# Two MLPs behind a packed attention: a pair of PSUM banks of their own for the small products, their latest input first, loads tied to steps

## The chip, the cores and the metric

The kernel runs on one core of a Trainium2 chip. The number that counts is the device time of one execution in microseconds (us): the median of three runs of the kernel before is 851.89 us (850.17 to 852.31). TensorE multiplies matrices (PE in the profile), VectorE (DVE) and ScalarE (ACT) work on elements, GpSimd (POOL) issues a few DMAs and SyncE (SP) most of them. PSUM, which TensorE writes its products to, has eight banks; a bank here holds 128 partitions by 512 float32 numbers.

## The reference

```python
def sm_attn(qq, kk, vv):
    s = scale * np.matmul(qq, kk.transpose(0, 1, 3, 2))
    s = s - np.max(s, axis=-1, keepdims=True)
    a = np.exp(s)
    a = a / (np.sum(a, axis=-1, keepdims=True) + 1e-09)
    return np.matmul(a, vv)
p_packed = sm_attn(p, k, v)             # p: [4, 8, 32, 64]; q, k, v: [4, 8, 576, 64], float32
x = sm_attn(q, p_packed, p_packed)      # then packed to [2304, 512]
h = x @ w_in                            # 512 x 2048, float64 weights
x = (h * np.tanh(log1p(exp(h)))) @ w_out   # 2048 x 512: first MLP (Mish)
h = x @ w_in2                           # second MLP, the same shapes, ELU
out = np.where(h > 0.0, h, np.exp(np.minimum(h, 0.0)) - 1.0) @ w_out2
```

## The kernel before

**The large products.** Each of the four large matrix products is made as three products of parts (high by high, high by low, low by high), so that its precision is that of float32. The float64 weights arrive as pairs of 32-bit words. ACT (L135) and DVE (L138, L143, L148) decode them into float32, and `split` (L163 on ACT, L165 or L167 on DVE) makes the high and the low part. The stages follow one another: `startup` (attention of batch 0, first decoded weights), `mixture1` (the first MLP, 128 steps of 288 tokens by 128 hidden columns), `mixture2` (the second MLP, 80 steps, 16 for each block of 512 or at last 256 tokens). Step i of mixture1 is `gemm1(i)` (L445 to L447, 6 products), `mish(i)` (ACT L454 and L455, DVE L456) and `gemm2(i-2)` (L473 to L475, 12 products). Step i of mixture2 is `gemm3` (L536 to L538, 12 products) one step ahead, its ELU (ACT L540, DVE L541 and L542, then the split L163 and L165), and `gemm4` (L559 to L561).

**The small products.** Attention and the folds run on TensorE in tiles of 32x32 or 64x32 of its array, where several instructions for different tiles go side by side. For each batch b they are: `scores1` (L244, p by k; kT from DVE's transpose L224), `transpose_a1` (L288), `packed` (L313, then L335 or L337), `scores2` (L354, q by the packed values; qT from L224 as well) and four times `fold` (L414), which multiplies the packed values into 512 columns of the first MLP's weights. What a fold leaves is the left operand G[b, c] of gemm1, so that gemm1 needs only the softmax of scores2 (`turn_s`, `exps`, `norm`, `back`: tiles x, a2t, a2h, a2l) on its other side. A small product has a "pe" step and "post" steps, which read its PSUM tile.

**PSUM before.** `ps_a` holds two tiles of two banks, the accumulators of gemm2 and gemm4. `ps_h` holds four single banks, taken in turn by gemm1, by gemm3 and, two at a time, by `pm()` for every small product.

**What sets the order.** Two tracks, `att` and `fol`, hold the small products of batches 1 to 3 with the step from which each may start; at each step of mixture1 a track takes one step of its current product. Loads of k, v and q of the next batch are issued at fixed steps (LOADOFF), folds of batch 0 at the steps of F0. The order in which the code emits instructions is not the order on the engines: a scheduler of the framework, with a model of times, reorders them as their inputs, tiles and banks come free. A tile of the `small` pool (nine slots) or of `up` (29) must be released by its last reader before it is taken again.

Of the kernel before, what the change touches and what calls it, by code (L numbers as in the profile page):

```python
# [20 lines left out]
    F0=[0, 14, 19],  # L21
# [8 lines left out]
    LOADOFF=[-2, 4, 0, 6, 11, 12],  # L30
# [13 lines left out]
def kernel(  # L44
# [19 lines left out]
    NK = DFF // 128  # L64
# [15 lines left out]
    ps_h = ctx.enter_context(tc.tile_pool(name="ps_h", bufs=4, space=bass.MemoryType.PSUM))  # L80
# [10 lines left out]

    def pm():
        if starting[0]:
            turn[0] += 1
            if turn[0] % 2:
                t = ps_a.tile([128, 2, 512], F32, tag="acc", name="pm")
                return [t[:, 0, :], t[:, 1, :]]
        return [ps_h.tile([128, 512], F32, tag="h", name="pm") for _ in range(2)]
# [135 lines left out]
    def scores1(b, s):  # L234
        d = {}

        def pe():
            ps = d["ps"] = pm()
            for x in range(2):
                for g in range(4):  # L240
                    kg = kT[b, g].rearrange("p e s -> p (e s)").rearrange("p (j x t) -> p j x t", x=2, t=32)
                    for th in range(2):
                        r = 64 * s + 32 * th
                        nc.tensor.matmul(  # L244
                            out=ps[th][32 * g:32 * g + 32, 0:HALF],
                            lhsT=pT[r:r + 32, b * 4 + g, x, :],
                            rhs=kg[r:r + 32, :, x, :],
                            start=(x == 0),
                            stop=(x == 1),
                        )  # L250
            if s:
                for g in range(4):
                    kT.pop((b, g))

        def post1():
            sm = d["sm"] = st.tile([128, 6], F32, tag="sm", name="sm")
            for e in range(2):
                nc.vector.reduce_max(out=sm[:, 2 + e:3 + e], in_=d["ps"][e][:, 0:HALF], axis=AX.X)
            nc.vector.tensor_scalar(
                out=sm[:, 1:2], in0=sm[:, 2:3], scalar1=sm[:, 3:4], scalar2=-scale, op0=ALU.max, op1=ALU.mult  # L260
            )
            e1 = E1[b, s] = small([128, 2, HALF], F32, f"e1_{b}_{s}")
            for e in range(2):
                nc.scalar.activation(
                    out=e1[:, e, :].rearrange("p (t j) -> p j t", t=32),
                    in_=d["ps"][e][:, 0:HALF].rearrange("p (j t) -> p j t", t=32), func=ACTF.Exp,
                    bias=sm[:, 1:2], scale=scale, accum_out=sm[:, 4 + e:5 + e],
                )

        def post2():  # L270
            sm = d["sm"]
            rs = RS[b, s] = st.tile([128, 2], F32, tag="rs", name="rs")
            nc.vector.tensor_scalar(
                out=rs[:, 0:1], in0=sm[:, 4:5], scalar1=sm[:, 5:6], scalar2=1e-9, op0=ALU.add, op1=ALU.add
            )
            nc.vector.reciprocal(out=rs[:, 1:2], in_=rs[:, 0:1])

        return [pe, post1, post2]
# [26 lines left out]
    def packed(b, s):  # L305
        d = {}

        def pe():
            a1 = A1T.pop((b, s))
            ps = d["ps"] = pm()  # L310
            for i, w, _, _ in CHUNKS:
                for g in range(4):
# [32 lines left out]
    def scores2(b):  # L345
# [3 lines left out]
        def pe(e):  # L349
            ps = d[e] = pm()  # L350
            for g in range(4):
# [34 lines left out]
        def back(s):  # L386
# [11 lines left out]
            lambda: (turn_s(1), exps(0)),  # L398
# [7 lines left out]
    def fold(b, c):  # L406
        d = {}

        def pe():
            ps = d["ps"] = pm()  # L410
            for g in range(4):
# [116 lines left out]
    def gemm3(j, kk):  # L528
        n = blocks[j][1]
        h = ps_h.tile([128, 512], F32, tag="h", name="h2")  # L530
        hp = h[:, 0:n]
# [46 lines left out]
    def attention_steps(b):  # L578
        st = [transpose_heads(kt_in, kT, b, g, "kT") for g in range(4)]
        st += [scores1(b, s) for s in range(2)]  # L580
        st += [transpose_a1(b, s, P["EVA"][s]) for s in range(2)]
        st += [packed(b, s) for s in range(2)]
        st += [transpose_heads(qt_in, qT, b, g, "qT") for g in range(4)]
        return st + [scores2(b)]
# [37 lines left out]
    def startup():  # L622
# [26 lines left out]
        def filler(m):  # L649
# [8 lines left out]
        hk, hq, s2 = at[0:4], at[10:14], at[14]  # L658
# [5 lines left out]
            6, hq[0][0], hq[1][0], hq[2][0], hq[3][0], s2[0], s2[1], s2[2], s2[3], 8, f0[0], f0[1],  # L664
            s2[4], s2[5], 45,
# [10 lines left out]
    class Track:  # L676
# [7 lines left out]

        def start(self, i):
# [4 lines left out]
    def mixture1():  # L690
# [3 lines left out]
        for b in range(1, B):  # L694
# [7 lines left out]
            for off, f in (  # L702
                (P['LOADOFF'][0], lambda b=b: load_kt(k, kt_in, b, 0, "k")),
                (P['LOADOFF'][1], lambda b=b: load_vt(b, 0)),
                (P['LOADOFF'][2], lambda b=b: load_kt(k, kt_in, b, 1, "k")),
                (P['LOADOFF'][3], lambda b=b: load_vt(b, 1)),
                (P['LOADOFF'][4], lambda b=b: load_kt(q, qt_in, b, 0, "q")),
                (P['LOADOFF'][5], lambda b=b: load_kt(q, qt_in, b, 1, "q")),
            ):
                at.setdefault(max(a0 - 1 + off, 0), []).append(f)  # L710
# [4 lines left out]
        fold0 = {F0[c - 1]: fold(0, c) for c in range(1, 4)}  # L715
        fposts = []
        for i in range(NA + LAG):
            for f in fposts:
                f()
            fposts = []  # L720
# [3 lines left out]
            att.posts()  # L724
            if i < NA:
# [7 lines left out]
            if i in fold0:  # L733
                fold0[i][0]()
                fposts.append(fold0[i][1])
            if FAST0 <= i < 2 * NK:
                att.posts()
                if not fol.cur and not att.cur:
# [5 lines left out]
            if not fol.cur and not att.cur:  # L744
# [77 lines left out]
```

## Time and profile before

| what | value |
|---|---|
| median of three runs | 851.89 us (850.17 to 852.31) |
| the profiled execution | 850.69 us |
| its span, from first to last instruction | 848.6 us |
| PE busy | 794.7 us (94%) |
| DVE busy | 441.4 us (52%) |
| ACT busy | 355.5 us (42%) |
| mean granted clock of TensorE | 0.963 of full speed |
| mean DMA rate | 94 GB/s |

The profile page divides the span into 40 slices. TensorE is nearly always busy from the fifth slice on, and has most of its idle time in the first four. The busy time of the second to the fourth slice is what DVE, ACT and the loads have to do before there is a first large product. The page's fifth part lists groups of instructions by line. The product lines of the four large products carry nearly all of TensorE's time: L473 to L475 appear 512 times each, L536 to L538 320 times and L559 to L561 288 times.

### The profile page before, as it was taken

The page shows a single profiled execution, that of the slowest core. Times are in us where ns is not written, and L with a number is a line of the kernel's source. Part 1 is how long each engine was busy: PE and PEld are TensorE (multiplying, and loading weights), DVE is VectorE, ACT ScalarE, POOL GpSimd, SP SyncE. Part 2 cuts the span into 40 slices and gives each one's busy share as a digit, 9 for nine tenths or more (in the row PEclk, how much of TensorE's full clock was granted, in tenths as well). Part 3 has the DMA queues.
Part 4 walks back from the last instruction along what each step waited for, and adds up shares of the span by engine and source line. Part 5 has one row for each costly group of instructions (what it writes and reads, how often), then busy time and mean ns, then how long its engine had stood idle before and what let it go on. Part 6 is the DMA issues. An engine that isn't in the chain of part 4 may idle for free.

```text
span 848.6 us, 12983 instructions
## 1 busy us (share of the span) xinstructions
PE 794.7 (94%) x5172; PEld 672.4 (79%) x5172; DVE 441.4 (52%) x860; ACT 355.5 (42%) x678; POOL 14.1 (2%) x30
## 2 busy tenths in 40 slices
PE   4508899999999999999998999999999999999997
PEld 3207687799878898699996888888888888888886
DVE  2789787823463335545617999523352334333443
ACT  1355665636374545556436565322231223222222
POOL 0000000000000000000000000000000000000000
PEclk7658899999999999999999999999999999999999
DMA  8996483443223332522106453200020001000000
GB/s 208 292 392 187 151 254 82 111 168 56 79 81 125 93 50 93 184 78 76 43 12 209 144 172 96 92 12 1 1 75 13 1 1 37 26 1 1 31 21 25
DMA packets 86044, 80.01 MB, mean 94 GB/s; under 512 B 63712, under 2 KB 68320, under 8 KB 85984
## 3 DMA queue, kind: packets, MB, share of 16 engines
q1 hardware_dynamic: 76704, 69.16, 26.3%
q0 software_dynamic: 2432, 8.91, 2.8%
q10 hardware_dynamic: 6848, 1.11, 0.7%
q8 instruction: 40, 0.66, 0.3%
q14 instruction: 20, 0.16, 0.1%
HBM read 65.54 MB, written 13.63 MB: 93 GB/s over the span
## 4 chain that ended last, share of the span: by engine, by line
PE 48%; issue 39%; DMA 4%; DVE 3%; ACT 2%; SPq 2%; POOL 1%; ACTq 0%; POOLq 0%; DVEq 0%
PE o L559 8%; PE o L560 8%; PE o L561 8%; PE h L536 7%; PE h L538 7%; PE h L537 7%; DMA raw_w1o<-in_moe_w_out_dram 1%; DMA v<-in_v_dram 1%; POOL y_dr L489 1%; DMA pr<-in_p_dram 1%; SPq L201 1%; DVE dec L143 1%; SPq L111 1%; PE acc L474 1%; DMA raw_w2i<-in_moe_w_in_dram 1%
## 5 line engine op out<-in xcount | busy, mean ns | idle before, releaser
L474 PE MATMUL acc<-gl,w1oh 128*128 128x288 f32 x512 | 151.0, 297 | 0.0
L475 PE MATMUL acc<-gh,w1ol 128*128 128x288 f32 x512 | 150.0, 295 | 0.0
L473 PE MATMUL acc<-gh,w1oh 128*128 128x288 f32 x512 | 148.8, 301 | 0.3
L536 PE MATMUL h<-yh,w2ih 128*128 128x512 f32 (+1 forms) x320 | 117.0, 369 | 2.7 <-ACT yh L163 1.4
L537 PE MATMUL h<-yl,w2ih 128*128 128x512 f32 (+1 forms) x320 | 118.0, 369 | 0.0
L538 PE MATMUL h<-yh,w2il 128*128 128x512 f32 (+1 forms) x320 | 117.3, 368 | 0.0
L559 PE MATMUL o<-w2oh,gh 128*128 128x512 f32 x288 | 112.5, 390 | 0.7 <-ACT ob L212 0.7
L560 PE MATMUL o<-w2ol,gh 128*128 128x512 f32 x288 | 112.4, 390 | 0.0
L540 ACT ACTIVATE t<-h 128x512 f32<-128x512 f32 (+1 forms) x80 | 44.2, 553 | 156.0 <-PE h L538 155.8
L456 DVE TENSOR_TENSOR gl<-t,gh 128x288 fp32r<-128x288 f32 x128 | 57.8, 453 | 96.6 <-ACT gh L455 96.4
L445 PE MATMUL h<-a2h,gh 128*128 128x288 f32 x256 | 80.8, 317 | 27.8 <-ACT a2h L163 23.9
L541 DVE TENSOR_SCALAR t<-t 128x512 f32<-128x512 f32 (+1 forms) x80 | 32.0, 399 | 142.6 <-ACT t L540 142.6
L473 PEld LDWEIGHTS acc<-gh,w1oh 128*128 128x128 f32 x512 | 95.2, 190 | 11.8 <-issue 8.3
L561 PE MATMUL o<-w2oh,gl 128*128 128x512 f32 x288 | 104.1, 390 | 0.0
L474 PEld LDWEIGHTS acc<-gl,w1oh 128*128 128x128 f32 x512 | 96.7, 189 | 4.9 <-issue 1.9
L475 PEld LDWEIGHTS acc<-gh,w1ol 128*128 128x128 f32 x512 | 96.6, 189 | 0.0
L454 ACT ACTIVATE t<-h 128x288 f32<-128x288 f32 x128 | 52.1, 409 | 102.2 <-PE h L447 100.2
L445 PEld LDWEIGHTS h<-a2h,gh 128*128 128x128 f32 x256 | 49.3, 193 | 45.2 <-ACT a2h L163 25.1
L163 ACT ACTIVATE gh<-t 128x512 fp32r<-128x512 f32 (+1 forms) x80 | 47.0, 587 | 73.2 <-DVE t L542 51.5
L446 PE MATMUL h<-a2l,gh 128*128 128x288 f32 x256 | 77.2, 302 | 0.1
L447 PE MATMUL h<-a2h,gl 128*128 128x288 f32 x256 | 76.8, 301 | 0.0
L165 DVE TENSOR_TENSOR gl<-t,gh 128x512 fp32r<-128x512 f32 (+1 forms) x80 | 51.0, 637 | 43.7 <-ACT gh L163 43.6
(96 smaller groups left out, 1144.7 us busy)
## 6 DMA issues: line engine op xcount, KB each, us to landing
w1r<-w_dr SPq DMA_DIRECT2D x24, 512.0 KB, 4.7
raw_w1i<-in_moe_w_in_dram SPq DMA_DIRECT2D x16, 512.0 KB, 6.9
raw_w1o<-in_moe_w_out_dram SPq DMA_DIRECT2D x16, 512.0 KB, 10.2
raw_w2i<-in_moe_w_in_dram SPq DMA_DIRECT2D x16, 512.0 KB, 4.8
raw_w2o<-in_moe_w_out_dram SPq DMA_DIRECT2D x16, 512.0 KB, 4.4
k<-in_k_dram SPq DMA_DIRECT2D x16, 288.0 KB, 5.8
y_dr<-y POOLq DMA_DIRECT2D x16, 288.0 KB, 2.6
out_dram<-ob SPq DMA_DIRECT2D x18, 256.0 KB, 2.0
```

Source lines behind the costliest of these rows:

```text
L445: nc.tensor.matmul(out=hp, lhsT=wh, rhs=xh, start=(kt == 0), stop=False)
L446: nc.tensor.matmul(out=hp, lhsT=wh, rhs=xl, start=False, stop=False)
L447: nc.tensor.matmul(out=hp, lhsT=wl, rhs=xh, start=False, stop=(kt == 1))
L473: nc.tensor.matmul(out=o, lhsT=wh[:, cs], rhs=gh, start=first, stop=False)
L474: nc.tensor.matmul(out=o, lhsT=wh[:, cs], rhs=gl, start=False, stop=False)
L475: nc.tensor.matmul(out=o, lhsT=wl[:, cs], rhs=gh, start=False, stop=last)
L536: nc.tensor.matmul(out=hp, lhsT=wh, rhs=xh, start=(i == 0), stop=False)
L537: nc.tensor.matmul(out=hp, lhsT=wh, rhs=xl, start=False, stop=False)
L538: nc.tensor.matmul(out=hp, lhsT=wl, rhs=xh, start=False, stop=(i == 3))
L559: nc.tensor.matmul(out=o, lhsT=gh[:, ts], rhs=wh, start=(kk == 0), stop=False)
L560: nc.tensor.matmul(out=o, lhsT=gh[:, ts], rhs=wl, start=False, stop=False)
L561: nc.tensor.matmul(out=o, lhsT=gl[:, ts], rhs=wh, start=False, stop=(kk == NK - 1))
```

## The change

It has six parts. (1) `ps_h` shrinks from four banks to two. The two freed banks become one tile, `ps_p`, that `pm()` gives to every small product after startup; in startup two turns of three take an accumulator of `ps_a`. `gemm3` uses all four banks through `hbank`: of four steps the first two take the two banks of ps_h, the third takes the pair and its first half, the fourth its second half. (2) The loops over the four head pairs in scores1, packed, scores2 and fold run from 3 down to 0. (3) The loads of v are issued with the second pe step of scores1, those of q with the pe steps of packed; LOADOFF is gone. (4) scores2 is two products for the track instead of one: the transposes out of PSUM in the first, the softmax in the second. (5) The folds of batch 0 stand in the `fol` track, at steps 0, 12 and 17, and a fold may also start ahead of gemm1. (6) `att` doesn't start a product while a fold is due.

```diff
-    ps_h = ctx.enter_context(tc.tile_pool(name="ps_h", bufs=4, space=bass.MemoryType.PSUM))
+    ps_h = ctx.enter_context(tc.tile_pool(name="ps_h", bufs=2, space=bass.MemoryType.PSUM))
+    ps_p = ctx.enter_context(tc.tile_pool(name="ps_p", bufs=1, space=bass.MemoryType.PSUM))
...
     def pm():
-        if starting[0]:
-            turn[0] += 1
-            if turn[0] % 2:
-                t = ps_a.tile([128, 2, 512], F32, tag="acc", name="pm")
-                return [t[:, 0, :], t[:, 1, :]]
-        return [ps_h.tile([128, 512], F32, tag="h", name="pm") for _ in range(2)]
+        turn[0] += 1
+        if starting[0] and turn[0] % 3:
+            t = ps_a.tile([128, 2, 512], F32, tag="acc", name="pm")
+        else:
+            t = ps_p.tile([128, 2, 512], F32, tag="pm", name="pm")
+        return [t[:, 0, :], t[:, 1, :]]
+
+    spare = []
+
+    def hbank(n):
+        if n % 4 < 2:
+            return ps_h.tile([128, 512], F32, tag="h", name="h2")
+        if n % 4 == 2:
+            spare.append(ps_p.tile([128, 2, 512], F32, tag="pm", name="h2"))
+            return spare[0][:, 0, :]
+        return spare.pop()[:, 1, :]
...
# in scores1, packed, scores2 and fold
-                for g in range(4):
+                for g in (3, 2, 1, 0):
...
         return [
             lambda: pe(0),
             lambda: (turn_s(0), pe(1)),
-            lambda: (turn_s(1), exps(0)),
+            lambda: turn_s(1),
+        ], [
+            lambda: exps(0),
             lambda: exps(1),
             lambda: (norm(0), back(0)),
             lambda: (norm(1), back(1)),
...
# gemm3
-        h = ps_h.tile([128, 512], F32, tag="h", name="h2")
-        hp = h[:, 0:n]
+        hp = hbank(j * NK + kk)[:, 0:n]
...
# attention_steps
+        for s in range(2):
+            x = scores1(b, s)
+            if s:
+                x[0] = then(x[0], lambda: load_vt(b, 0), lambda: load_vt(b, 1))
+            st.append(x)
...
+            x = packed(b, s)
+            x[0] = then(x[0], lambda s=s: load_kt(q, qt_in, b, s, "q"))
...
+        st += scores2(b)
...
# mixture1, inside the loop over the steps
             fol.posts()
             att.posts()
+            if not fol.cur and not att.cur:
+                fol.start(i)
             if i < NA:
                 gemm1(i)
...
-                if not fol.cur and not att.cur:
+                if not fol.cur and not att.cur and not fol.due(i):
                     att.start(i)
```

How this moves instructions on TensorE in the first small product of batch 1 (pm is its PSUM tile, kT1_0 to kT1_3 are the transposed heads of k, acc and h1 the tiles of gemm2 and gemm1). Before, the first scores1 begins like this:

```order
L473 MATMUL acc0_612<-gh1_669,w1oh4_0_520 128x288
L473 MATMUL acc1_613<-gh1_669,w1oh4_0_520 128x288
L244 MATMUL pm_833<-kT1_0_692,pT_94 32x288
L244 MATMUL pm_834<-kT1_0_692,pT_94 32x288
L244 MATMUL pm_833<-kT1_1_719,pT_94 32x288
L244 MATMUL pm_834<-kT1_1_719,pT_94 32x288
L474 MATMUL acc0_612<-gl1_670,w1oh4_0_520 128x288
L475 MATMUL acc0_612<-gh1_669,w1ol4_0_521 128x288
L473 MATMUL acc0_612<-gh1_669,w1oh4_0_520 128x288
```

It goes on in three further pieces with ten to twelve large products between them. In the changed kernel it stands in one piece, with a large product ahead of it and behind it:

```order
L461 MATMUL h1_692<-a2h0_431,gl0_1_563 128x288
L256 MATMUL pm_821<-kT1_3_783,pT_97 32x288 x2
L256 MATMUL pm_821<-kT1_2_750,pT_97 32x288 x2
L256 MATMUL pm_821<-kT1_1_717,pT_97 32x288 x2
L256 MATMUL pm_821<-kT1_0_690,pT_97 32x288 x2
L256 MATMUL pm_821<-kT1_3_783,pT_97 32x288 x2
L256 MATMUL pm_821<-kT1_2_750,pT_97 32x288 x2
L256 MATMUL pm_821<-kT1_1_717,pT_97 32x288 x2
L256 MATMUL pm_821<-kT1_0_690,pT_97 32x288 x2
L459 MATMUL h1_719<-a2h0_431,gh0_1_562 128x288
```

There all 16 instructions, two to a row, follow one another; kT1_3 comes first.

On VectorE in startup, the softmax behind the second scores (x0_0 and x0_1 are its scores, w1v and w1ol decoded weights, gl0_0 a part of the first fold). Before, from the last transposes out of PSUM:

```order
L368 STREAM_TRANSPOSE x0_1_380<-pm_383 128x288
L167 SCALAR_TENSOR_TENSOR gl0_0_422<-pm_412,gh0_0_421 128x512
L375 TENSOR_REDUCE mx2_394<-x0_0_378 128x18
L375 TENSOR_REDUCE mx2_398<-x0_1_380 128x18
L167 SCALAR_TENSOR_TENSOR w1ol0_0_449<-dec_447,w1oh0_0_448 128x512
L148 SCALAR_TENSOR_TENSOR w1v1_0_459<-raw_w1i0_1_196,dec_458 128x512
L148 SCALAR_TENSOR_TENSOR w1v1_2_467<-raw_w1i2_1_198,dec_466 128x512
L376 TENSOR_TENSOR x0_0_378<-x0_0_378,mx2_394 128x576
L167 SCALAR_TENSOR_TENSOR gl0_0_422<-pm_412,gh0_0_421 128x512
L376 TENSOR_TENSOR x0_1_380<-x0_1_380,mx2_398 128x576
L138 TENSOR_SCALAR dec_474<-raw_w1i1_1_200 128x512
L138 TENSOR_SCALAR dec_482<-raw_w1i3_1_202 128x512
```

In the changed kernel, from the same place:

```order
L380 STREAM_TRANSPOSE x0_1_380<-pm_382 128x288
L387 TENSOR_REDUCE mx2_393<-x0_0_378 128x18
L387 TENSOR_REDUCE mx2_397<-x0_1_380 128x18
L388 TENSOR_TENSOR x0_0_378<-x0_0_378,mx2_393 128x576
L388 TENSOR_TENSOR x0_1_380<-x0_1_380,mx2_397 128x576
L393 TENSOR_REDUCE sm2_426<-x0_0_378 128x18
L393 TENSOR_REDUCE sm2_437<-x0_1_380 128x18
L394 TENSOR_SCALAR sm2_426<-sm2_426 128x18
L394 TENSOR_SCALAR sm2_437<-sm2_437 128x18
L395 RECIPROCAL sm2_426<-sm2_426 128x18
L179 SCALAR_TENSOR_TENSOR gl0_0_421<-pm_411,gh0_0_420 128x512
L395 RECIPROCAL sm2_437<-sm2_437 128x18
```

The steps of the softmax follow one another up to the reciprocal and beyond, and the two parts of the fold and the decodes that stood between them come later.

On TensorE where mixture2 begins (h2 is the tile of gemm3; yh and yl are its right operand). Before, this is where the fourth gemm3 ends and the fifth begins:

```order
L536 MATMUL h2_5429<-yh0_1_5100,w2ih2_0_4289 128x512
L537 MATMUL h2_5429<-yl0_1_5101,w2ih2_0_4289 128x512
L538 MATMUL h2_5429<-yh0_1_5100,w2il2_0_4290 128x512
L536 MATMUL h2_5462<-yh0_0_5096,w2ih0_1_5107 128x512
L537 MATMUL h2_5462<-yl0_0_5097,w2ih0_1_5107 128x512
L538 MATMUL h2_5462<-yh0_0_5096,w2il0_1_5108 128x512
```

In the changed kernel the fifth, h2_5421, stands behind the third, h2_5356:

```order
L549 MATMUL h2_5356<-yh0_1_5060,w2ih2_0_4249 128x512
L550 MATMUL h2_5356<-yl0_1_5061,w2ih2_0_4249 128x512
L551 MATMUL h2_5356<-yh0_1_5060,w2il2_0_4250 128x512
L549 MATMUL h2_5421<-yh0_0_5056,w2ih0_1_5067 128x512
L550 MATMUL h2_5421<-yl0_0_5057,w2ih0_1_5067 128x512
L551 MATMUL h2_5421<-yh0_0_5056,w2il0_1_5068 128x512
```

The fourth, which takes the second half of tile h2_5356, comes behind the first products of the second gemm4 (gh2_5338):

```order
L572 MATMUL o0_5342<-w2oh0_0_4294,gh2_5338 128x512
L573 MATMUL o0_5342<-w2ol0_0_4295,gh2_5338 128x512
L572 MATMUL o1_5343<-w2oh0_0_4294,gh2_5338 128x512
L573 MATMUL o1_5343<-w2ol0_0_4295,gh2_5338 128x512
L549 MATMUL h2_5356<-yh0_0_5056,w2ih0_0_4204 128x512
L574 MATMUL o0_5342<-w2oh0_0_4294,gl2_5339 128x512
```

So three gemm3 products instead of four are done before the first bank is needed again.

## Rows read from the trace of the kernel before

**Rows 1.** Stretches of 20 us: busy us and count by engine, PEclk, DMA share, GB/s

```profile
40.00:60.00 20.00, 0.00 (x0) 0.00 (x0) 15.73 (x33) 10.66 (x18) 1.06 (x2) 0.52 1.03 411
60.00:80.00 20.00, 15.14 (x87) 12.54 (x88) 19.38 (x36) 12.17 (x24) 0.00 (x0) 0.71 0.63 198
...
100.00:120.00 20.00, 18.32 (x157) 15.48 (x157) 15.23 (x33) 14.15 (x27) 1.20 (x2) 0.86 0.59 171
...
240.00:260.00 20.00, 19.86 (x147) 13.89 (x146) 11.65 (x23) 11.85 (x25) 0.00 (x0) 1.00 0.28 93
...
380.00:400.00 20.00, 20.00 (x154) 20.00 (x153) 13.44 (x28) 13.39 (x30) 0.00 (x0) 1.00 0.36 114
```

**Rows 2.** Waits of PE: us in total, times, longest us

```profile
PE h L445 <- ACT a2h L163: 23.9, 1, 23.9
PE h L445 <- ACT t L454: 3.0, 2, 2.7
```

**Rows 3.** Timeline of PE at scores1 of batches 1 and 2: start, us, instruction

```profile
84.53 0.69 PE L244 MATMUL pm<-kT,pT 32*32 32x288 f32 x8
85.15 0.40 PE L474 MATMUL acc<-gl,w1oh 128*128 128x288 f32 x1
85.39 0.30 PE L475 MATMUL acc<-gh,w1ol 128*128 128x288 f32 x1
85.52 0.29 PE L473 MATMUL acc<-gh,w1oh 128*128 128x288 f32 x1
...
86.57 0.42 PE L473 MATMUL acc<-gh,w1oh 128*128 128x288 f32 x2
86.92 0.68 PE L244 MATMUL pm<-kT,pT 32*32 32x288 f32 x6
...
195.11 1.20 PE L244 MATMUL pm<-kT,pT 32*32 32x288 f32 x32
196.24 0.40 PE L445 MATMUL h<-a2h,gh 128*128 128x288 f32 x1
```

**Rows 4.** Timeline of PE at three folds

```profile
113.23 1.06 PE L414 MATMUL pm<-w1v,pt 64*32 64x512 f32 x8
114.22 0.40 PE L473 MATMUL acc<-gh,w1oh 128*128 128x288 f32 x1
...
165.69 1.09 PE L414 MATMUL pm<-w1r,pt 64*32 64x512 f32 x16
166.71 0.40 PE L445 MATMUL h<-a2h,gh 128*128 128x288 f32 x1
...
241.56 1.91 PE L414 MATMUL pm<-w1r,pt 64*32 64x512 f32 x4
243.40 0.40 PE L474 MATMUL acc<-gl,w1oh 128*128 128x288 f32 x1
```

**Rows 5.** Timeline of PE at a piece of scores2 of batch 1

```profile
135.83 1.15 PE L354 MATMUL pm<-qT,pt 64*32 64x288 f32 x6
136.91 0.40 PE L474 MATMUL acc<-gl,w1oh 128*128 128x288 f32 x1
```

**Rows 6.** Timelines of ACT and DVE in startup

```profile
43.55 0.65 ACT L135 ACTIVATE raw_w1o<-raw_w1o 128x512 f32<-128x512 f32 x1 [1.63 <-DMA raw_w1o<-in_moe_w_out_dram]
...
44.71 0.69 DVE L167 SCALAR_TENSOR_TENSOR gl<-pm,gh 128x512 fp32r<-128x512 f32 x1 [4.27 <-ACT gh L163]
...
65.84 0.76 DVE L165 TENSOR_TENSOR a2l<-a2t,a2h 128x576 fp32r<-128x576 f32 x1
```

**Rows 7.** Timelines of DVE and PE at the start of mixture2

```profile
460.47 0.68 DVE L542 SCALAR_TENSOR_TENSOR t<-h,t 128x512 f32<-128x512 f32 x1
...
459.32 0.39 PE L537 MATMUL h<-yl,w2ih 128*128 128x512 f32 x1
459.55 0.39 PE L538 MATMUL h<-yh,w2il 128*128 128x512 f32 x1
461.20 0.50 PE L536 MATMUL h<-yh,w2ih 128*128 128x512 f32 x1 [1.26 <-DVE t L542]
```

More of the change, by code (lines that the diff above doesn't have):

```diff
@@ L20 @@
     DEC1=[14, 26],
-    F0=[0, 14, 19],
+    F0=[0, 12, 17],
     LEAD=2,
@@ L29 @@
     RELOFF=-7,
-    LOADOFF=[-2, 4, 0, 6, 11, 12],
     NU=29,
@@ L311, in pe @@
             for i, w, _, _ in CHUNKS:
-                for g in range(4):
+                for g in (3, 2, 1, 0):
                     nc.tensor.matmul(
@@ L350, in pe @@
             ps = d[e] = pm()
-            for g in range(4):
+            for g in (3, 2, 1, 0):
                 for s in range(2):
@@ L410, in pe @@
             ps = d["ps"] = pm()
-            for g in range(4):
+            for g in (3, 2, 1, 0):
                 for s in range(2):
@@ L578, in attention_steps, with then, both @@
     def attention_steps(b):
-        st = [transpose_heads(kt_in, kT, b, g, "kT") for g in range(4)]
-        st += [scores1(b, s) for s in range(2)]
+        def then(f, *loads):
+            def both():
+                f()
+                for x in loads if b else ():
+                    x()
+            return both
+        st = [transpose_heads(kt_in, kT, b, g, "kT") for g in range(4)]
+        for s in range(2):
[3 more added lines that the diff above has]
+            st.append(x)
         st += [transpose_a1(b, s, P["EVA"][s]) for s in range(2)]
-        st += [packed(b, s) for s in range(2)]
+        for s in range(2):
+            x = packed(b, s)
+            x[0] = then(x[0], lambda s=s: load_kt(q, qt_in, b, s, "q"))
+            st.append(x)
         st += [transpose_heads(qt_in, qT, b, g, "qT") for g in range(4)]
-        return st + [scores2(b)]
+        st += scores2(b)
+        return st
     NA = 2 * B * NK
@@ L657, in startup @@
         at = attention_steps(0)
-        hk, hq, s2 = at[0:4], at[10:14], at[14]
+        hk, hq, s2 = at[0:4], at[10:14], at[14] + at[15]
         sc, ta, pk = at[4:6], at[6:8], at[8:10]
@@ L663, in startup @@
             ta[0][0], ta[0][1], ta[1][0], ta[1][1], 4, pk[0][0], pk[0][1], pk[0][2], pk[1][0], pk[1][1], pk[1][2],
-            6, hq[0][0], hq[1][0], hq[2][0], hq[3][0], s2[0], s2[1], s2[2], s2[3], 8, f0[0], f0[1],
-            s2[4], s2[5], 45,
+            6, hq[0][0], hq[1][0], hq[2][0], hq[3][0], s2[0], s2[1], s2[2], s2[3], s2[4], 8, f0[0], f0[1],
+            s2[5], s2[6], 45,
         ]
@@ L683, in posts, with due @@
                 self.cur.popleft()()
+        def due(self, i):
+            return bool(self.q) and self.q[0][0] <= i
         def start(self, i):
@@ L701, in mixture1 @@
                 at.setdefault(i0 + NK + 4 * c + P['RELOFF'], []).append(lambda c=c: reload_w1i(c))
[L702 to L710, printed above, removed]
+            for x in range(2):
+                at.setdefault(max(a0 - 3 + 2 * x, 0), []).append(lambda b=b, x=x: load_kt(k, kt_in, b, x, "k"))
         w2q = deque(interleave("w2"))
@@ L714, in mixture1 @@
         tile2 = 2 * (B - 1) * NK + P['T2']
-        fold0 = {F0[c - 1]: fold(0, c) for c in range(1, 4)}
-        fposts = []
+        for c in (3, 2, 1):
+            fol.q.appendleft((F0[c - 1], fold(0, c)))
         for i in range(NA + LAG):
-            for f in fposts:
-                f()
-            fposts = []
             for f in at.get(i, ()):
@@ L732, in mixture1 @@
                 decode_w1(m)
-            if i in fold0:
-                fold0[i][0]()
-                fposts.append(fold0[i][1])
             if FAST0 <= i < 2 * NK:
                 att.posts()
-                if not fol.cur and not att.cur:
+                if not fol.cur and not att.cur and not fol.due(i):
                     att.start(i)
@@ L743, in mixture1 @@
                 fol.start(i)
-            if not fol.cur and not att.cur:
+            if not fol.cur and not att.cur and not fol.due(i):
                 att.start(i)
```

## The prediction

> **What bounds the kernel now.** I read the busy time by stretches first. From 120 us on, nearly every stretch of 20 us shows TensorE busy for 20 us at a granted clock of 1.00; 380 to 400 is the pure case, where 154 large products fill 20.00 us, 0.130 us each [rows 1]. Before that it is different: TensorE does nothing between 40 and 60, and between 60 and 80 VectorE is busy for 19.38 of 20 us while TensorE's clock stands at 0.71 [rows 1]. So there are two regimes: a start bound by VectorE and the loads (to about 120 us), then a long part in which only TensorE's own work and its own pauses count. The list of TensorE's waits says the same. One wait is large, 23.9 us for the first a2h; waits of gemm1 for a bank of h come to 3.0 us, in two places [rows 2].
>
> Then the timeline of TensorE, because busy does not mean useful. Small products go in sweeps over the tiles of the array, and a sweep costs about the same whether it is full or not. A piece of scores1 with 4 instructions (8 records, two to an instruction) begins at 84.53, the next large product at 85.15: 0.62 us. The whole of a scores1, 16 instructions, takes 1.13 us, from 195.11 to 196.24 [rows 3]. Half a fold takes 0.99 us (113.23 to 114.22), a whole one 1.02 (165.69 to 166.71) [rows 4]. A piece of scores2 with 6 instructions that meet twice on the same tile takes 1.08 us [rows 5]. And each return to the large products costs something: twelve of them stand between 85.15 and 86.92, which is 1.77 us where 12 x 0.130 would be 1.56: 0.2 us [rows 1, 3].
>
> **The change part by part.** Latest input first, and an own pair of banks. The scheduler places a small product when its first instruction can go, and cuts it where the next input or bank is not there yet; with the latest input in front it can only go whole. By the two orders the pieces in mixture1, after the first large product, are:
> - folds: 23 pieces before, 15 after. 8 x 0.99 = 7.9 us less [rows 4].
> - scores2: 11 pieces, of which about five are double sweeps at 1.08 and six single ones at 0.6, 9.2 us, to 7 single ones, 4.2: 5.0 to 5.4 less [rows 3, 5]; I take 5.3.
> - scores1: 13 to 9 pieces. The first of batch 1 goes from four pieces (about 2.5 us) to 1.13, the first of batch 2 from two (1.7) to 1.13: 2.0 less [rows 3]. The first of batch 3 stays cut in four.
> - returns to large products: 21 fewer by the orders (the pieces of transpose_a1 included, and those that now stand back to back), x 0.2 = 4.2 us [rows 3].
>
> Together 19.4 us of TensorE's time. By batch it is 7.1 for batch 2, 5.5 for batch 3 (its scores1 and scores2 stay cut in part), and the remaining 6.8 for the folds of batch 0 and for batch 1. Batches 2 and 3 lie where TensorE is the only bound, so 12.6 us count in full; I bound them by 10 and 13.5. Of batch 1 a part lies where VectorE is late (up to about 120 us), so there a shorter TensorE only waits longer: bounds 0 and 6.8, I take 3.
>
> Startup. Between the last transpose of the scores out of PSUM and the second a2l, VectorE's order before holds 25 instructions of decodes and folds, the changed one 11. Fourteen instructions at some 0.6 us are about 8 us by which a2l, and with it the first steady gemm1, can come forward from 65.84 us [rows 6]. But the decodes are not gone: gemm2 needs them, and VectorE is full from 60 to 80 [rows 1]. What is truly gained is idle time of VectorE: 4.27 us, in which it waits for a gh that stands on ScalarE behind a decode whose load arrives at 43.55 [rows 6]; in the new order that part of the fold comes after the reciprocals. So the gain lies between 0 and 8 us; I take 4, the row's idle time.
>
> Fewer banks for gemm1. With two instead of four, gemm1 of step i+2 needs the bank that mish of step i reads. Before, it waited twice in all [rows 2]. In the new order 30 to 38 large products, 3.9 to 5 us, stand between the end of one gemm1 and the start of the next but one, which covers ScalarE's read of one tile unless ScalarE is late. Nothing is excluded: the bounds are 0 and 4 us (a little over twice the two waits of before would be 6, but those had small products taking banks as well); I take 1.2. The new place of the loads is priced at nothing by itself. They stand on SP behind the step that they follow, and the q of batch 1 now waits on SP for the first packed of that batch, with a w1o load queued behind it, whose decode a fold's gh follows on ScalarE. The cover is all the large products between packed and the second scores2 of that batch; were it gone, what gemm1 would wait is held by the 4 above.
>
> Start of mixture2. Before, four gemm3 products run before the first bank is needed again; TensorE then stops once, for 1.26 us up to 461.20, because VectorE's L542 of the first runs only at 460.47 [rows 7]. In the new order the fifth gemm3 stands behind the third, and the fourth, in the second half of the pair, later. TensorE arrives 12 products earlier at the same wait; a product takes 0.23 us (459.32 to 459.55) [rows 7], so the wait is 2.8 us longer. Later the seventh gemm3 takes the pair again and needs L542 of the fourth, late in a VectorE that is full there: 0 to 2.8 us more, I take 1.4. Nothing comes back afterwards, since the same products must run. Bounds 0 (the scheduler's times are pessimistic and L542 comes early) and 8 (both waits, twice); I take 4.2.
>
> The sum: -4.0 -3.0 -12.6 +1.2 +4.2 = -14.2. From the profiled execution's 850.69 that is 836.5; the median of three runs is 1.2 us above that execution, so 837.7. All low ends give about 823, all high ends 853.
>
> **Rivals.**
> (A) The single pair becomes the bound, and the kernel gets slower. Each small product must wait until ScalarE and VectorE have read the one before it. For: a fold that found no bank in the trace of before took 1.84 us for one piece instead of 0.99, a wait of 0.85 [rows 4], with four banks to choose from. Mixture1 has 39 small products; from 17 such waits on (17 x 0.85 = 14.4) the gain is gone, with 25 it is 21 us lost against the other terms: about 859. Against: in the new order most small products have 27 or more large ones ahead of them, 3.5 us. Only in batch 1 do two packed and a fold follow each other directly.
> The Trainium skill has a rule on this side: "TensorEngine Tiling (Array Packing)", section "PSUM Bottleneck", says that tiling makes TensorE faster and not the emptying of PSUM, which may then become the limit. The trace bears it out in one piece of the folds of batch 2 [rows 4] and not in the others that stand there; by the rule alone (A) would be the forecast.
> (B) VectorE bounds everything up to 120 us, and the start and batch 1 give nothing. For: 19.38 of 20 us busy [rows 1]. Then -12.6 + 1.2 + 4.2 = -7.2: 844.7.
> (C) The whole 8 us of the start and all of batch 1 are kept and mixture2 loses only the first 2.8: -8 - 6.8 - 12.6 + 1.2 + 2.8 = -23.4: 828.5. For: between 100 and 120 TensorE is busy 18.32 of 20 us [rows 1], so little of its time there is spare, and less work on it could show at once. Against: the decodes still have to come.
> (D) TensorE's clock falls in new short pauses. For: between 100 and 120 it was busy 18.32 us and granted 0.86 [rows 1]. Against: between 240 and 260 it paused too, and the clock stayed at 1.00 [rows 1]. If all nine stretches from 180 to 360 lost 0.14 of 20 us each, that is 25 us: about 863.
> The Trainium skill, "TensorE: Matmul & The Clock Gate", section "A second HAM failure mode: psum-queue depth-cycling", tells of a kernel whose clock went up and down because it cycled through PSUM banks with small pauses; the stretch from 240 to 260, with its bank wait, does not show that here.
>
> **How the numbers follow.** The forecast has 0.55, with its own range 830 to 844; (B) 0.18; (C) 0.13; (A) 0.11; (D) 0.03. Two executions of this kernel differ by up to 0.3% (850.17 to 852.31), so 0.3%, 2.6 us, is what can be told from no change: 849.3 to 854.4. (A) spreads around break-even: of its 0.11, 0.05 end within the bound, 0.06 above it; (D) ends above it or, in part, within. From the upper edge of (B) comes another 0.02 within the bound. So faster 0.85, same 0.07, slower 0.08. The range from 824 to 851 leaves out some 0.05 below, from (C), and 0.12 above, from (A) and (D).
>
> **What would show it.** Right: in the profile after, whole folds of about 1.02 us and scores2 of about 0.6 us in one piece each; the first a2h wait a few us shorter than 23.9; mixture1 (first gemm1 to last gemm2) shorter by 12 to 20 us; one idle time of TensorE of about 4 us at the start of mixture2, for L542. Wrong: waits of a pm tile for ScalarE or VectorE in the list of TensorE's waits that add up to over 14 us (A); the first a2h earlier, but TensorE waiting for w1ol or for mish between 60 and 100 (B); a clock under 1.00 after 180 us (D). If the pieces stay cut in the trace as before, the first term fails, and with it the forecast.

## The result, and the profile after

The changed kernel takes 839.22 us (median of four runs, 838.91 to 839.93), the kernel before 851.72 in the same runs: a ratio of 0.9857, 95% interval 0.984 to 0.9874. The forecast was 837.7, its own range 830 to 844. The span of the profiled execution fell from 848.6 to 836.8 us.

Small sums hide large terms, so I set up an account from both traces: for each stretch, its length less 0.1302 us for each large product of gemm1 and gemm2 in it. What is left is small products, returns to large products, and idle time. The stretches are cut at the first gemm1 and at the first scores1 of each batch; mixture2 is counted against 0.2267 us a product. TensorE's clock, the granted clock of the stretches, has two levels, so a stretch of 20 us at 0.87 spent some 5 us at half speed.

| stretch | before | after | difference | predicted |
|---|---|---|---|---|
| up to the first gemm1 | 62.05 | 54.76 | -7.3 | |
| from there to scores1 of batch 1 | 8.94 | 12.05 | +3.1 | start together: -4.0 |
| batch 1 | 31.32 | 24.62 | -6.7 | -3.0 |
| batch 2 | 21.25 | 14.79 | -6.5 | -7.1 |
| batch 3 to the end of mixture1 | 23.26 | 19.31 | -3.9 | -5.5 |
| new waits for h in mixture1 | | in the rows above | | +1.2 |
| mixture2, first 400 products | 3.70 | 12.27 | +8.6 | +4.2 |
| mixture2, the rest | | | +0.9 | 0 |
| sum | | | -11.8 | -14.2 |

The stretches of 20 us of the kernel after, which answer to [rows 1]:

```profile
40.00:60.00 20.00, 3.83 (x12) 2.94 (x12) 16.53 (x33) 12.02 (x20) 0.33 (x1) 0.50 1.03 410
60.00:80.00 20.00, 16.86 (x129) 13.83 (x129) 20.00 (x39) 11.47 (x26) 1.30 (x2) 0.82 0.67 215
80.00:100.00 20.00, 20.00 (x181) 19.03 (x182) 17.80 (x43) 15.18 (x32) 1.07 (x2) 1.00 0.42 124
100.00:120.00 20.00, 16.36 (x198) 13.83 (x205) 16.56 (x35) 12.54 (x27) 1.07 (x2) 0.96 0.80 264
120.00:140.00 20.00, 20.00 (x152) 17.75 (x137) 14.74 (x28) 9.55 (x20) 0.00 (x0) 0.87 0.60 176
...
240.00:260.00 20.00, 20.00 (x168) 18.00 (x167) 9.55 (x18) 10.28 (x24) 0.54 (x1) 1.00 0.40 145
```

From 60 to 80 VectorE is full now (20.00). Yet from 80 to 100 TensorE is busy throughout. Between 100 and 140 the clock falls once more (0.96 and 0.87), which is 3.4 us of 40 lost; the kernel before lost as much between 80 and 120 (0.97, and 0.86 in [rows 1]).

TensorE's waits after, beside [rows 2]:

```profile
PE h L459 <- ACT a2h L175: 15.9, 1, 15.9
...
PE h L549 <- DVE t L555: 5.8, 3, 3.6
...
PE acc L487 <- ACT w1oh L175: 2.2, 1, 2.2
...
PE h L459 <- ACT t L468: 1.0, 3, 0.6
```

The first is 8.0 us shorter. gemm1's waits for a bank of h come to 1.0 us, with two banks, where four gave 3.0 [rows 2]. The second row is new in size: gemm3 waiting for L555, the third time at 505.63 for 0.64 us. The third row is new too: the earlier gemm2 waits for a decoded w1oh, at 68 us. (Lines have moved: gemm1 is L459 to L461 now, gemm2 L487 to L489, gemm3 L549 to L551, and L555 is the L542 of before.)

Whole pieces on TensorE: a scores1, a scores2 (L366) and a fold (L428), each with the large product behind it, against [rows 3 to 5]:

```profile
77.74 1.20 PE L256 MATMUL pm<-kT,pT 32*32 32x288 f32 x32
78.87 0.40 PE L459 MATMUL h<-a2h,gh 128*128 128x288 f32 x1
...
147.97 0.72 PE L366 MATMUL pm<-qT,pt 64*32 64x288 f32 x16
148.62 0.40 PE L489 MATMUL acc<-gh,w1ol 128*128 128x288 f32 x1
...
152.37 1.09 PE L428 MATMUL pm<-w1r,pt 64*32 64x512 f32 x16
153.39 0.40 PE L461 MATMUL h<-a2h,gl 128*128 128x288 f32 x1
```

1.13, 0.65 and 1.02 us, in one piece each. In mixture1 the trace has 15 pieces of folds for 23, 7 of scores2 for 11, 9 of scores1 for 13.

VectorE in startup, against [rows 6]:

```profile
42.22 1.42 DVE L388 TENSOR_TENSOR x<-x,mx 128x576 f32<-128x576 f32 x2
47.12 1.41 DVE L393 TENSOR_REDUCE sm<-x 128x18 f32<-128x576 f32 x2 [3.47 <-ACT x L389]
...
48.83 0.63 DVE L179 SCALAR_TENSOR_TENSOR gl<-pm,gh 128x512 fp32r<-128x512 f32 x1
...
58.01 0.76 DVE L177 TENSOR_TENSOR a2l<-a2t,a2h 128x576 fp32r<-128x576 f32 x1
```

The wait for gh is gone, and 3.47 us of waiting for the exps has come instead; the second a2l ends 7.8 us earlier all the same.

Where packed of batch 1 stands, all through the one pair (the place that rival A named; pv and pt are the packed values of one half and of both):

```profile
113.31 0.90 PE L325 MATMUL pm<-v,a1t 128*32 128x64 f32 x40
116.12 0.30 PE L349 MATMUL pm<-ident,pv 128*64 128x128 f32 x1 [1.90 <-DVE pv L338]
117.27 0.90 PE L325 MATMUL pm<-v,a1t 128*32 128x64 f32 x40 [0.86 <-DVE pt L226]
118.66 0.69 PE L347 MATMUL pm<-ident,pv 128*64 128x128 f32 x2 [0.49 <-DVE pv L338]
119.73 1.96 PE L428 MATMUL pm<-w1v,pt 64*32 64x512 f32 x16 [0.39 <-DVE pt L226]
121.63 0.61 PE L487 MATMUL acc<-gh,w1oh 128*128 128x288 f32 x1
```

Four waits, 3.64 us, and no large product between them. Two of them, 2.39 us, are for pv, which VectorE makes of the first part of the same packed; they are not waits for a bank. The other two, 1.25 us, stand behind the copy to pt that reads the pair out (L226), and of these the fold's 0.39 needs that pt itself as well. It is the only such place in mixture1.

The start of mixture2 on TensorE, against [rows 7]:

```profile
427.11 0.98 PE L549 MATMUL h<-yh,w2ih 128*128 128x512 f32 x3 [1.45 <-ACT yh L175]
...
437.38 0.39 PE L551 MATMUL h<-yh,w2il 128*128 128x512 f32 x1
439.32 0.50 PE L549 MATMUL h<-yh,w2ih 128*128 128x512 f32 x1 [1.56 <-DVE t L555]
...
459.58 0.61 PE L549 MATMUL h<-yh,w2ih 128*128 128x512 f32 x1 [3.64 <-DVE t L555]
459.99 0.63 PE L550 MATMUL h<-yl,w2ih 128*128 128x512 f32 x1
```

VectorE and ScalarE ahead of the two waits:

```profile
438.58 0.68 DVE L555 SCALAR_TENSOR_TENSOR t<-h,t 128x512 f32<-128x512 f32 x1
...
454.42 0.68 ACT L147 ACTIVATE raw_w2o<-raw_w2o 128x512 f32<-128x512 f32 x1 [1.63 <-DMA raw_w2o<-in_moe_w_out_dram]
455.51 1.56 ACT L553 ACTIVATE t<-h 128x512 f32<-128x512 f32 x3
```

The first gemm3 of the kernel before, which [rows 7] does not have:

```profile
448.40 1.21 PE L536 MATMUL h<-yh,w2ih 128*128 128x512 f32 x4 [1.44 <-ACT yh L163]
```

The stretches of the kernel after:

```profile
420.00:440.00 20.00, 16.71 (x82) 13.78 (x82) 11.24 (x20) 11.09 (x19) 1.08 (x2) 0.91 0.51 187
...
460.00:480.00 20.00, 20.00 (x83) 16.45 (x82) 19.58 (x38) 10.58 (x19) 0.00 (x0) 0.92 0.50 169
```

The first wait is hardly longer than before, 1.56 for 1.26 us; the second, for the pair, is 3.64; three exps (L553) run only at 455.51, behind a decode on ScalarE that waited for its load. In both stretches the granted clock is low for a while: products begin 0.41 us apart behind the second (459.58 to 459.99), where 0.23 is the rule [rows 7], and the stretch has 83 products instead of 90. The 0.92 of that stretch is 1.6 us.

### The profile page after: what moved, and what is told of

It reads as the page before. It is cut to its first block, busy times and chain, and to the rows that moved or that the text cites. A ratio compares the mean times of both kernels' runs of the same rounds, so it can differ in the third digit from the quotient of the medians.

```text
span 836.8 us, 12979 instructions
## 1 busy us (share of the span) xinstructions
PE 778.2 (93%) x5172; PEld 669.6 (80%) x5172; DVE 438.1 (52%) x860; ACT 348.1 (42%) x674; POOL 14.3 (2%) x30
## 5 line engine op out<-in xcount | busy, mean ns | idle before, releaser
L489 PE MATMUL acc<-gh,w1ol 128*128 128x288 f32 x512 | 151.7, 298 | 0.9 <-DVE w1ol L179 0.9
L487 PE MATMUL acc<-gh,w1oh 128*128 128x288 f32 x512 | 148.5, 299 | 2.2 <-ACT w1oh L175 2.2
L549 PE MATMUL h<-yh,w2ih 128*128 128x512 f32 (+1 forms) x320 | 117.8, 372 | 7.3 <-DVE t L555 5.8
L551 PE MATMUL h<-yh,w2il 128*128 128x512 f32 (+1 forms) x320 | 119.0, 372 | 0.0
L574 PE MATMUL o<-w2oh,gl 128*128 128x512 f32 x288 | 108.2, 389 | 0.0
L487 PEld LDWEIGHTS acc<-gh,w1oh 128*128 128x128 f32 x512 | 96.3, 191 | 6.2 <-ACT w1oh L175 2.4
L489 PEld LDWEIGHTS acc<-gh,w1ol 128*128 128x128 f32 x512 | 97.5, 191 | 3.9 <-issue 2.6
L553 ACT ACTIVATE t<-h 128x512 f32<-128x512 f32 (+1 forms) x80 | 42.3, 552 | 138.2 <-PE h L551 133.7
L459 PE MATMUL h<-a2h,gh 128*128 128x288 f32 x256 | 77.3, 304 | 16.9 <-ACT a2h L175 15.9
L461 PE MATMUL h<-a2h,gl 128*128 128x288 f32 x256 | 76.7, 301 | 0.0
L549 PEld LDWEIGHTS h<-yh,w2ih 128*128 128x128 f32 x320 | 60.7, 190 | 19.5 <-DVE t L555 7.4
```

The costliest lines, as they stand in the source:

```text
L459: nc.tensor.matmul(out=hp, lhsT=wh, rhs=xh, start=(kt == 0), stop=False)
L461: nc.tensor.matmul(out=hp, lhsT=wl, rhs=xh, start=False, stop=(kt == 1))
L487: nc.tensor.matmul(out=o, lhsT=wh[:, cs], rhs=gh, start=first, stop=False)
L489: nc.tensor.matmul(out=o, lhsT=wl[:, cs], rhs=gh, start=False, stop=last)
L549: nc.tensor.matmul(out=hp, lhsT=wh, rhs=xh, start=(i == 0), stop=False)
L551: nc.tensor.matmul(out=hp, lhsT=wl, rhs=xh, start=False, stop=(i == 3))
```

## The experiments

Theory 1 is the prediction's: the latest input in front keeps a small product whole. Theory 2: it is the pair, taken as one tile, that does. All ratios are to the kernel before in the same runs, with 95% intervals.

**Loops undone.** In the changed kernel:

```diff
# in scores1, packed, scores2 and fold
-                for g in (3, 2, 1, 0):
+                for g in range(4):
```

> The changed kernel with one part undone: the loops over the head pairs run 0 to 3 again, the own pair of banks stays. Theory 1 (the prediction's): what keeps small products in one piece is that the latest input comes first. Then folds and scores go back to about the pieces of before (23 and 24 in mixture1), TensorE has 15 to 19 us more to do there, and the time is 850 or more. Theory 2 (rival): it is the pair taken as one tile, which holds the first instruction back until both banks are free and so lets the inputs gather. Then folds stay at about 15 pieces of 1.0 us, only scores2 is cut a little (about 9 pieces for 7), and the time is 840 to 843.

Measured: 844.83 us, 0.9913 (0.9897 to 0.993). The time lies between the two numbers; the pieces are theory 2's. Folds stay whole: 14 pieces in mixture1 (one more fold lies ahead of the first gemm1), 13 of 1.02 us and one of 1.89 at the lower clock, scores2 9, scores1 10; the small products come to 43.2 us there, against 42.9 in the changed kernel. So the loops are not what makes the folds whole. What was lost lies early. The first gemm1 comes at 63.89, 9.1 us later; by the account 2.6 of these are left when batch 1 begins, since less is lost behind the first gemm1. And batch 1 loses 28.8 us for 24.6, with 5.9 us of waits for 4.1 and 10.2 us at the lower clock for 6.8.

```profile
63.89 0.85 PE L459 MATMUL h<-a2h,gh 128*128 128x288 f32 x2 [3.41 <-ACT a2h L175]
```

**Loops alone,** in the kernel before:

```diff
# in scores1, packed, scores2 and fold
-                for g in range(4):
+                for g in (3, 2, 1, 0):
```

> The kernel before with one part alone: the loops over the head pairs run 3 to 0; four single banks shared as before. Theory 1: nearly all of the gain of mixture1 is there (folds in 15 or so pieces of 1.0 us, 15 us and more less) and mixture2 loses nothing: 830 to 836. Theory 2: folds stay at 22 or 23 pieces; scores2 goes from 11 to about 5 pieces and scores1 from 13 to about 10, together with the returns some 8 to 10 us less: 842 to 846.

Measured: 840.03 us, 0.9854 (0.9835 to 0.9873). Neither number was right: as fast as the whole change, but not by whole folds, which stay at 22 pieces and 23.8 us (26.8 before). scores2 goes to 5 pieces and 4.8 us (9.6). The first gemm1 comes at 52.94, 9.1 us earlier, but 16.1 us are lost from there to scores1 of batch 1 (8.9 before), so only 1.9 us of it are left; batches 1 to 3 give 12.9 us. At the start of mixture2 gemm3 waits once:

```profile
PE h L445 <- ACT a2h L163: 16.6, 2, 12.9
...
PE h L536 <- DVE t L542: 3.3, 1, 3.3
```

**The pair as two tiles.** In the changed kernel, for pm and hbank alike:

```diff
-            t = ps_p.tile([128, 2, 512], F32, tag="pm", name="pm")
+            return [ps_p.tile([128, 512], F32, tag="pm%d" % x, name="pm") for x in range(2)]
         return [t[:, 0, :], t[:, 1, :]]
...
+        return ps_p.tile([128, 512], F32, tag="pm%d" % (n % 4 - 2), name="h2")
```

> The changed kernel, but the pair is two single-bank tiles that are taken and released apart, for small products and for gemm3 alike. Theory 1: mixture1 stays as in the changed kernel (whole pieces, since the loops still run 3 to 0); in mixture2 the second wait for the pair (3.6 us, then 3.4 us at half clock) goes: 832 to 836. Theory 2: folds and scores2 are cut again (about 23 and 11 pieces), mixture1 gives back 13 to 18 us; even with 5 to 7 us won in mixture2 the time is 845 to 852.

Measured: 850.47 us, 0.9981 (0.9967 to 0.9995), as theory 2 had it. 23 pieces of folds, with the loops still from 3 down. The trace shows where they are cut, at the border of the two banks (lines 3 lower here):

```profile
166.00 1.06 PE L425 MATMUL pm<-w1r,pt 64*32 64x512 f32 x8
166.99 0.40 PE L458 MATMUL h<-a2h,gl 128*128 128x288 f32 x1
...
167.72 1.06 PE L425 MATMUL pm<-w1r,pt 64*32 64x512 f32 x8
...
168.18 0.58 ACT L172 ACTIVATE gh<-pm 128x512 fp32r<-128x512 f32 x1
```

Half a fold, four large products, another half; ScalarE reads the first bank from 168.18, while the second half still runs (to 168.78), so each half fills one bank. Mixture1 gives back 12.8 us (what is not large products: 70.8 to 83.5).

**The banks shared as before,** everything else as changed:

```diff
-    ps_h = ... bufs=2 ...
-    ps_p = ... bufs=1 ...
+    ps_h = ... bufs=4 ...
...
-            t = ps_p.tile([128, 2, 512], F32, tag="pm", name="pm")
+            return [ps_h.tile([128, 512], F32, tag="h", name="pm") for _ in range(2)]
...
     def hbank(n):
...
+        return ps_h.tile([128, 512], F32, tag="h", name="h2")
```

> The changed kernel with the banks of before: four single banks shared by gemm1, gemm3 and the small products; loops, loads, tracks and scores2 as changed. Theory 1: whole pieces, mixture1 as in the changed kernel or a little better, mixture2 without its 9 us of loss: 829 to 834. Theory 2: folds cut again (23 pieces, 8 to 10 us more in mixture1 with the returns), scores2 whole (5 pieces), mixture2 as before: 838 to 843.

Measured: 839.95 us, 0.9869 (0.9839 to 0.9899): theory 2's number, with 23 pieces of folds and 5 of scores2. Equal to the changed kernel: there the pair wins 10.1 us up to the first gemm3 (427.11 for 437.19) and loses 8.3 from there on.

**Four single banks for mixture2.** The order of mixture1 is that of the changed kernel:

```diff
+    first = ExitStack()
+    ps_h = first.enter_context(tc.tile_pool(name="ps_h", bufs=2, ...))
+    ps_p = first.enter_context(tc.tile_pool(name="ps_p", bufs=1, ...))
...
-    mixture2(*mixture1())
+    left = mixture1()
+    first.close()
+    ps_2 = [ctx.enter_context(tc.tile_pool(name="ps_2", bufs=4, ...))]
+    mixture2(*left)
...
-        hp = hbank(j * NK + kk)[:, 0:n]
+        hp = ps_2[0].tile([128, 512], F32, tag="h2", name="h2")[:, 0:n]
```

> The changed kernel, with the two PSUM pools closed after mixture1 and four single banks opened in their place for gemm3; the order of mixture1 is the same, instruction for instruction. Theory 1: what mixture2 loses against before (7.6 us by its 120th product, in two waits for a bank and the half clock behind each) comes from fewer products ahead and from the two halves of the pair being tied together; then 6 to 8 us come back: 831 to 834. Theory 2 (rival): the loss comes from loads and decodes of the second MLP's weights, which stand ahead of the exps on ScalarE, and mixture2 merely begins earlier against them; then 837 to 839.

Measured: 829.91 us, 0.9759 (0.9738 to 0.978), the lowest time of all and clear of the changed kernel's interval. Theory 1 of this run holds, and a little more came back than it said; TensorE's products of mixture1 stand in the same order in both traces. The stretches:

```profile
420.00:440.00 20.00, 17.91 (x93) 14.89 (x92) 11.46 (x20) 11.40 (x19) 1.08 (x2) 1.00 0.53 188
440.00:460.00 20.00, 20.00 (x90) 16.54 (x89) 20.00 (x39) 12.25 (x22) 0.00 (x0) 1.00 0.42 132
460.00:480.00 20.00, 20.00 (x90) 16.58 (x89) 19.57 (x38) 12.46 (x22) 0.00 (x0) 1.00 0.55 184
```

No stretch under 1.00, and one wait for a bank, 0.6 us. Mixture2's loss by its 400th product is 2.95 us, less than before (3.70).

**The smaller parts, each undone alone** in the changed kernel. The loads at fixed steps:

```diff
-                x[0] = then(x[0], lambda: load_vt(b, 0), lambda: load_vt(b, 1))
...
-            x[0] = then(x[0], lambda s=s: load_kt(q, qt_in, b, s, "q"))
...
+                at.setdefault(a0 + 4 + 2 * x, []).append(lambda b=b, x=x: load_vt(b, x))
+                at.setdefault(a0 + 12 + 2 * x, []).append(lambda b=b, x=x: load_kt(q, qt_in, b, x, "q"))
```

> The changed kernel with the loads of v and q at fixed steps again (v four and six, q twelve and fourteen steps after the start of the batch's attention) instead of behind scores1 and packed. Theory 1: the loads were priced at nothing: 838 to 841. Theory 2: the tied loads carry the part of batch 1's gain that the prediction did not see (3.7 us): 842 to 845.

scores2 as one product of the track:

```diff
-            lambda: turn_s(1),
-        ], [
-            lambda: exps(0),
+            lambda: (turn_s(1), exps(0)),
...
```

> The changed kernel with scores2 as one product of the track again, its softmax steps holding the track. Theory 1: the two halves together are one pipeline in which TensorE's order hardly moves: 838 to 841. Theory 2: the split lets the next fold start during the softmax; without it folds come late and gemm1 waits for G in batches 1 to 3: 842 or more.

The folds of batch 0 outside the track:

```diff
-            fol.q.appendleft((F0[c - 1], fold(0, c)))
+        fold0 = {F0[c - 1]: fold(0, c) for c in range(1, 4)}
...
+            if i in fold0:
+                fold0[i][0]()
+                fposts.append(fold0[i][1])
```

> The changed kernel with the folds of batch 0 outside the track, at steps 0, 14 and 19 as before. Theory 1: same pieces, same time within 1.5 us: 838 to 841. Theory 2: their order against scores1 of batch 1 carries the unforeseen 3.7 us of batch 1: 842 to 845.

Measured: loads 838.24 (0.9851, 0.9833 to 0.987), scores2 840.62 (0.9877, 0.9857 to 0.9897), folds 842.74 (0.9899, 0.988 to 0.9918). The first two are the changed kernel within the intervals. The folds are about 0.4% slower, theory 2's number but not its place: batch 1 has 25.9 us against 24.6, 2.6 us are lost before the first gemm1 (57.36 for 54.76), and mixture2's start takes 1.3 more.

**Loops and banks crossed,** with single banks in mixture2 throughout. Loops 0 to 3 with the pair, and loops 0 to 3 with shared banks (the edits above, combined):

> The changed kernel with four single banks for gemm3 and the loops over the head pairs running 0 to 3. With the loss of mixture2 out of the way, the order of the loops should be worth what it was with the pair in both stages (5 us, mostly a later start): 834 to 837. Rival: once mixture2 costs nothing the order of the loops no longer matters, because whole pieces come from the pair: 829 to 832.

> The changed kernel with neither of its two main parts: four single banks shared by all, loops 0 to 3; tracks, loads and the split of scores2 stay. If loops and pair carry nearly all of the change, this is the kernel before within 3 us: 849 to 855. Rival: loops, pair and the rest add up independently; then loops cost 5 us on top of the shared banks' 840: 843 to 847.

| | loops 0 to 3 | loops 3 to 0 |
|---|---|---|
| four shared banks | 0.991 (0.9885 to 0.9934) | 0.9869 (0.9839 to 0.9899) |
| pair for small products in mixture1 | 0.9837 (0.9808 to 0.9867) | 0.9759 (0.9738 to 0.978) |

With the other parts in place the pair is worth 0.7 to 1.1%, the loops 0.4 to 0.8%. The first expectation for the pair was too low (838.55), since mixture2 began less well in that order (a pause of 3.05 us, then low clock). The second came out at the rival's number (844.33): tracks, loads, split and startup's turns carry 0.9% together, although none of those undone alone shows more than 0.4%. But the parts do not add up: with the loops from 3 to 0 and shared banks, the same other parts are worth nothing (839.95 us with them, 840.03 without, in the same runs), and the loops alone were worth 1.5%.

**Both of the better-looking edits,** four banks in mixture2 and fixed loads:

> Four single banks for gemm3, and the loads of v and q at fixed steps. If tied loads are worth nothing: 828 to 831. If fixed steps save 1 us, as the run with them alone hinted: 827 to 829; if their 1.7 us more in batch 1 counts: 830 to 833.

Measured: 833.1 us, 0.9773 (0.9745 to 0.9801), at the upper end of the third number, and its interval overlaps that of the kernel with four banks alone. Batch 1 has 26.8 us for 25.1, and gemm3 waits longer:

```profile
PE h L539 <- DVE t L545: 2.9, 1, 2.9
```

So four single banks do not by themselves keep the start of mixture2 short: that wait was 0.6 us in the one order and 2.9 in the other. Against the same kernel with the pair in mixture2 they still save 0.8% here, 0.8% with the loops 0 to 3, and 1.0% in the best kernel.

**Startup's turns as before:**

```diff
-        if starting[0] and turn[0] % 3:
+        if starting[0] and turn[0] % 2:
```

> The changed kernel, its small products of startup taking an accumulator every second time, as before, instead of two times of three. Theory 1: the earlier first gemm1 (54.8 us, before 62.05) comes from the order of the loops, since without it the first gemm1 came at 63.9 with the same banks; then 838 to 841 and a first gemm1 near 55. Theory 2: it needs the third turn as well, because the second scores and the fold otherwise wait for the pair: first gemm1 at 58 or later and 842 to 846.

Measured: 836.63 us, 0.9835 (0.9817 to 0.9853); the first gemm1 at 53.15. The third turn is not needed for the earlier start: it came without the turns of three, and was lost without the loops from 3 to 0. The time, below theory 1's number, overlaps the changed kernel's interval.

## Why the prediction was right, and where its steps were not

**Right.** TensorE's own time bounds batches 2 and 3, and fewer pieces are worth what the sweeps' rows say: 12.6 less 1.2 us predicted, 10.4 measured. The counts of pieces came as forecast, and the cost of a whole piece too (the piece of scores2 with 6 records in [rows 5] has three instructions, not six; its time is right). gemm1's waits for a bank came to 1.0 us with two banks, 3.0 with four shared ones.

**Luck.** The forecast missed by 1.5 us only because its errors partly cancel: batch 1 gave 3.7 us more than forecast, mixture2 took 5.3 more. The start's -4.2 us net for -4.0 is luck as well. It was priced as the 4.27 us in which VectorE waited for gh, but 3.47 us of waiting for the exps came back in their place. What moved is work: from 34 us to the first scores1 of batch 1 VectorE is busy for 38.8 us, before for 44.3, and in batch 1 for 77.9, before for 71.3. Of the 7.3 us of the earlier first gemm1, 3.1 went back: TensorE waited 4.5 us for a2l, w1oh and w1ol (2.8 before), and spent 12.5 us at the lower clock (9.6).

**The step that failed: why pieces are whole.** "The scheduler places a small product when its first instruction can go ... with the latest input in front it can only go whole." With the loops undone the folds stayed whole; with the loops kept and the pair split into two tiles they were cut at the border of the banks. What joins a fold is the one tile for both banks. The order of the loops mattered elsewhere, and more than I had thought: alone it brings scores2 to 5 pieces and gives the whole change's time.

**Two terms mis-sized.** Batch 1: -3.0 predicted, -6.7 measured, at the bound of 6.8. I had held that VectorE is late up to 120 us; but between 80 and 100 TensorE is busy for 20.00 us, so what it was spared there counted. Waits and clock gave nothing in batch 1: 4.1 us of waits, before 2.9, and 6.8 us at the lower clock in each.
Mixture2: +4.2 predicted, +8.6 by the 400th product. For the first bank the mechanism held: from the first gemm3 to the bank's release TensorE lost 4.1 us against its usual step of 0.2267 us, before 1.9, so 2.1 more for +2.8. The wait shown grew by only 0.3, because TensorE itself was late at it by 1.8 us, through a late yl and the first low stretch (36 products took 10.5 us, before 48 took 11.4), and L555 came 0.6 us earlier behind the first product. By the trace it is L555 that sets 439.32, so this low stretch seems to have cost nothing; no run shows it. Instead of the one idle time of about 4 us there were two. The second wait was under-sized (1.4 for a measured 3.64); in the trace ScalarE has decodes with late loads ahead of the exps there. A third, of 0.64, and the clock behind the second, about 1.7 us, were not priced at all. Gaps between products beyond their usual step, 0.45 for a yl, 1.72, 3.8 and 0.8, and 3.4 for the clock make 10.2 of the 10.7 us lost from the first product of mixture2 to the 400th; before it was 2.1.

**The rivals.** (A) was real in one place of 39, at 0.86 to 1.25 us: with the pair as two tiles the waits for pv are there too (1.48 and 0.46 us), those behind L226 are not.
The rule of "TensorEngine Tiling (Array Packing)", "PSUM Bottleneck" in the Trainium skill, fits these waits behind L226 in batch 1 and no other place of mixture1 here.
(B) was wrong for batch 1; its sign, TensorE waiting for decoded weights between 60 and 100, came true at 68 to 70 us, for 3.1 us. (D) came true at the start of mixture2, at about 1.7 us net; behind the run of packed and fold in batch 1 the clock fell as well, for as long as in the kernel before, and between 180 and 420 us no stretch of the trace is under 1.00.

**Open.** What the remaining 0.9% consists of (the run with loops and banks both undone), and why it is gone once the loops run from 3 to 0, is not settled; of its parts only the folds' track showed a difference alone. That exps stand behind late loads is read from the trace; no run moved them. Why loops 3 to 0 bring the scores2 of shared banks to 5 pieces while two separate own banks leave 11 is not known either.

## What to carry to other kernels

If small products use two banks that are filled by separate instructions, take the two as one tile: a scheduler then can't start half a product, and half costs as much as the whole. Give each stage its own pools: against four shared banks the pair won 10.1 us up to the first gemm3 and cost 8.3 from there on, and a pool of its own for mixture2 gave that back. After a change of order, count the pieces in the trace before the cause is named; the loops alone and the whole change gave nearly the same time by different ways.

## What the hardware showed unexpectedly

A pause of TensorE early in mixture2 can cost half as much again behind it. In the fourteen traces, nine pauses between 2.74 and 4.24 us (from one product's start to the next, less the usual 0.23) occur in the first 400 products there; behind eight of them the granted clock goes to the lower of its two levels (1.2 GHz) for 3.4 us, some 1.7 us lost each time, and behind one (2.87 us) it does not. Of the shorter ones between 1.98 and 2.62 us, two were followed by it and three were not. And all fourteen traces have the same wait of 1.4 us just ahead of the first gemm3: in five of them, the changed kernel's among these, the clock falls 1.6 to 2.1 us behind that gemm3's start, in nine it does not, although the kernel with four single banks has the same products in the same order up to there. So the length of the pause alone does not decide it.
